# A fused attention and two-layer kernel: the first layer's w_out parts streamed from DRAM, and w_out2's combinations moved from GpSimd to VectorE

## The chip, the cores and the metric

The kernel runs on one core of one Trainium2 chip. The metric is the device time of one execution in microseconds (us). Of the kernel before, three runs are known: 1842.84, 1839.39 and 1833.98 us, median 1839.39. The trace is of one more execution, which took 1837.5 us.

The engines are named as in the profile: PE is TensorE's matmul side and PEld its weight loads, DVE is VectorE, ACT is ScalarE, POOL is GpSimd, SP is SyncE, which here does nothing but issue DMAs in order.

## The reference, cut to what matters

```python
# attention: 8 batches, 8 heads, 576 positions, head size 64; k and v averaged over groups of 8
k_p = k.reshape(B, H, Sp, pool, D).mean(axis=3)
v_p = v.reshape(B, H, Sp, pool, D).mean(axis=3)
attn = softmax(scale * q @ k_p.T)            # 576 x 72 for each head
x = (attn @ v_p)                             # rearranged to 4608 x 512

# first layer: w_in 512 x 2048, w_out 2048 x 512, stored as float64
h = x @ w_in
y = (h * np.cos(h)) @ w_out                  # 4608 x 512

# second layer: w_gate, w_val 512 x 1536, w_out2 1536 x 512, stored as float64
g = y @ w_gate
out = (g / (1 + np.exp(-g)) * (y @ w_val)) @ w_out2
```

## The kernel before, in words

**Precision.** Most matrix products are made of three fast matmuls: each operand is split into a high part (a copy rounded to the fast format, made by ScalarE) and a low part (the operand minus its high part, made by VectorE), and high x high, low x high and high x low are added up in PSUM. The weights come as float64 and are converted on VectorE by bit operations (the `cv_` functions).

**First layer.** The 4608 tokens are nine blocks (n = 0 to 8) of 512, the 2048 hidden columns sixteen groups (f = 0 to 15) of 128; one (n, f) is a *slot*, numbered i = 16 n + f, 144 in all. In a slot TensorE makes h (`pe_h`, L478 to L480, 12 matmuls of 512 columns) from x's parts `xhl` and w_in's parts `wa`, which stay on chip. ScalarE and VectorE then form h cos(h): `hs` (L487), `w` (L489, L490), sine and square (L501, L502), and the product (L505). `parts` splits it into `gh` (ScalarE, L517) and `gl` (VectorE, L519). Two slots later `pe_y` (L536 to L538, 12 matmuls) multiplies them with w_out's parts into four PSUM banks, `acc`. From slot 11 on w_out's row group f, which lies converted in two tiles `wo_raw` of eight groups each, is split again in every slot: the high part `woh` by ScalarE (`wo_high`, L495), the low part `wol` by VectorE (L518), each with two buffers in turn. At a block's last slot `x_split` splits the next block's x (4 copies on ScalarE, 4 subtractions on VectorE), and at the next block's second slot `y_out` sends y to DRAM (`y_dram`).

**Beside it.** Attention for the later batches, the sums over groups of 8 of k and v (GpSimd, L185 and L187, `do_raw`), and the conversion of the second layer's weights (36 units at the slots in `cv_slots`, stored to `w2_dram`) are placed in given slots.

**Second layer.** It is computed by a scheme of seven products (P1 to P7) on halves of rows and columns, which needs sums and differences of weight blocks. For w_out2 these are made once, in `gen_out`: for each of six pairs of 128-row tiles, `load` fetches them by eight strided DMAs (L676) into a tile `ow`; then come seven steps, one for a product: GpSimd makes the sum or difference (L701), ScalarE the high part (L703, L696), GpSimd the low part (L704; L697 and L698 for P4), and a DMA writes both to `wc_dram` (L706). Its 42 steps are written into the last block, four to a slot. The tiles `ow` lie in the places `tP6` and `tP7`, where operands of the second layer come later. `t_steps` and `gen_steps`, which make the first operands of the second layer, are in the last block too.

**What sets the order.** The program is written as one sequence, but a planner in the framework decides the order on each engine and on SP's queue when the kernel is built, by data and buffer dependencies and its own costs. An instruction can come earlier on its engine than it is written, as soon as its data and place are there. On the chip each engine then takes its list strictly in order; an instruction that waits holds up all behind it.

Of the kernel before, what the change touches and what calls it, by code (L numbers as in the profile page):

```python
# [8 lines left out]
F32 = mybir.dt.float32  # L9
F32R = mybir.dt.float32r  # L10
# [4 lines left out]
ALU = mybir.AluOpType  # L15
# [10 lines left out]
def fused_kernel(  # L26
# [18 lines left out]
    nc = tc.nc  # L45
# [56 lines left out]
    nc.gpsimd.memset(exp_bias, -896.0 * 2.0**23)  # L102
    nc.gpsimd.memset(magic, MAGIC)
    y_dram = dram.tile([KC, P, NT], F32, name="y_dram")
    w2_dram = dram.tile([3 * FF2 * DM // (P * TB), P, TB], F32, name="w2_dram")


# [16 lines left out]
    def split(hi, lo, src):  # L124
        nc.scalar.copy(hi, src)  # L125
        nc.vector.tensor_sub(lo, src, hi)  # L126
# [345 lines left out]
    def pe_h(s):  # L472
        n, f = s
        ps = psum.tile([P, TB], F32, name=f"h_{n}_{f}", tag="hg", bufs=2)
        j, o = f // 4, (f % 4) * P
        for c in range(KC):
            whi, wlo = wa[j, c][:, 0, o : o + P], wa[j, c][:, 1, o : o + P]
            nc.tensor.matmul(ps, whi, xhl[:, 0, c], start=c == 0, stop=False)  # L478
            nc.tensor.matmul(ps, whi, xhl[:, 1, c], start=False, stop=False)  # L479
            nc.tensor.matmul(ps, wlo, xhl[:, 0, c], start=False, stop=c == KC - 1)  # L480
        hps[s] = ps
# [9 lines left out]

    def wo_high(s):
        n, f = s
        a = wo[s] = p1w.tile([P, DM], F32R, name=f"woh_{n}_{f}", tag="woh", bufs=2)
        nc.scalar.copy(a, wo_raw[f // 8][:, f % 8])  # L495

    def cosine(s):
        n, f = s
        w, h = wsb[s], hsb.pop(s)

        nc.scalar.activation(w, w, AF.Sin, scale=PI)  # L501
        nc.scalar.activation(w, w, AF.Square, scale=SQRT2)  # L502
        if n:
            wo_high(s)
        nc.vector.scalar_tensor_tensor(out=w, in0=w, scalar=1.0, in1=h, op0=ALU.subtract, op1=ALU.mult, reverse0=True)  # L505

    def parts(s):
        n, f = s
        if n == 0 and f < Y32:
            return  # L510
        a = gh[s] = chain_tile("gh", f"gh_{n}_{f}", F32R)
        b = gl[s] = chain_tile("gl", f"gl_{n}_{f}", F32R)
        c = p1w.tile([P, DM], F32R, name=f"wol_{n}_{f}", tag="wol", bufs=2)
        w = wsb.pop(s)
        if not n:
            wo_high(s)
        nc.scalar.copy(a, w)  # L517
        nc.vector.tensor_sub(c, wo_raw[f // 8][:, f % 8], wo[s])  # L518
        nc.vector.tensor_sub(b, w, a)  # L519
        wo[s] = (wo[s], c)  # L520

    def pe_y(s):
        n, f = s
        if f == 0:
            acc[n] = [psum.tile([P, TB], F32, name=f"acc_{n}_{i}", tag=f"acc{i}") for i in range(4)]
        if n == 0 and f < Y32:
            g = wsb.pop(s)
            for i in range(KC):
                a = wo_raw[f // 8][:, f % 8, i * P : (i + 1) * P]
                nc.tensor.matmul(acc[n][i], a, g, start=f == 0, stop=f == NF1 - 1)  # L530
            return
        a, b = wo.pop(s)
        xh, xl = gh.pop(s), gl.pop(s)
        for i in range(KC):
            cols = slice(i * P, (i + 1) * P)
            nc.tensor.matmul(acc[n][i], a[:, cols], xh, start=f == 0, stop=False)  # L536
            nc.tensor.matmul(acc[n][i], a[:, cols], xl, start=False, stop=False)  # L537
            nc.tensor.matmul(acc[n][i], b[:, cols], xh, start=False, stop=f == NF1 - 1)  # L538
# [127 lines left out]
    def gen_out():  # L666

        work = {}

        def load(i):  # L670
            t = work[i] = pools2["a"].tile([P, 4, TB], F32, name=f"ow_{i}", tag=f"tP{6 + i % 2}")
            raw = t[:, :2].rearrange("p e (m c) -> p e m c", m=4)
            u = units.index(("o", i // 2, 2 * i))
            for e in range(2):
                for m in range(4):
                    nc.sync.dma_start(  # L676
                        raw[:, e, m].rearrange("p (a d) -> p a d", a=4),
                        w2_dram[u + e].rearrange("p (a m d) -> p m a d", a=4, m=4)[:, m],
                    )

        for i in range(NI):
            if i == 0:
                load(0)
            if i + 1 < NI:
                load(i + 1)
            t = work.pop(i)
            a11, a21, a12, a22 = (t[:, e, h * 256 : (h + 1) * 256] for e in range(2) for h in range(2))
            outs_ = [t[:, 2 + n].bitcast(F32R).rearrange("p (a c) -> p a c", a=2) for n in range(2)]
            for n, (prod, dst, x, y, op) in enumerate((
                ("P1", None, a11, None, None), ("P2", None, a12, None, None), ("P4", a11, None, None, None),  # L690
                ("P5", a22, a21, a22, ALU.add), ("P7", a21, a11, a21, ALU.subtract),
                ("P6", a11, a22, a11, ALU.subtract), ("P3", a12, a12, a11, ALU.subtract),
            )):
                o = outs_[n % 2]
                if prod == "P4":
                    nc.scalar.mul(o[:, 0], a22, -1.0)  # L696
                    nc.gpsimd.tensor_add(o[:, 1], a22, o[:, 0])  # L697
                    nc.gpsimd.tensor_scalar(o[:, 1], o[:, 1], -1.0, None, op0=ALU.mult)  # L698
                else:
                    if dst is not None:  # L700
                        nc.gpsimd.tensor_tensor(out=dst, in0=x, in1=y, op=op)  # L701
                        x = dst
                    nc.scalar.copy(o[:, 0], x)  # L703
                    nc.gpsimd.tensor_sub(o[:, 1], x, o[:, 0])  # L704
                k = NI * NQ + NJ * OUT_PRODUCTS.index(prod) + i // 2
                nc.sync.dma_start(  # L706
                    wc_dram[k].rearrange("p (a x) -> p a x", a=2)[:, i % 2], o.rearrange("p a c -> p (a c)").bitcast(F32)
                )
                yield

    def run(steps, m=1):
        for _ in range(m):
            next(steps, None)
# [332 lines left out]
    for i, s in enumerate(slots):  # L1046
        n, f = s
        if s == (NB - 1, 0):
            p1a.release()
            pools2["a"] = tc.alloc_tile_pool(name="p2a", bufs=1, reuse_waits="tile")  # L1050
            tsteps = t_steps(0)
            gsteps = None
        units1, units2 = units2, []
        if n == 0:
            if f % KC == 0:
                fill_to("i", f // KC, KC - 1)
            load_i(1)
        if i + 2 in cv_slots and i % NF1 != 1:
            w2_get()
        if f == 0 and i:  # L1060
            pe_y(slots[i - 2])
        pe_h(s)
        if n == 0:
            fill(4)
        turns(s)
        if 0 < i <= NF1:
            fill_to("o", 0, i - 1)
        if i:
            parts(slots[i - 1])
        if f == NF1 - 1 and n + 1 < NB:  # L1070
            x_split((n + 1) % 2)
        if n == 0:
            fill(2)
        for u in units1:
            cv_bias(u)
        if f == 1 and n:
            pe_y(slots[i - 2])
        run_slot(mids, i)
        if f > 1 or i == 1:
            if i >= 2:  # L1080
                pe_y(slots[i - 2])
        if n == 0:
            fill(2)
        cosine(s)
        if f == 1 and n:
            y_out(n - 1)
        for u in units1:
            nc.sync.dma_start(w2_dram[w2c], cv_val(u))
            w2c += 1
        run_slot(lates, i)  # L1090
        run_slot(exps, i)
        run_slot(norms, i)
        if n == 0:
            if i == 0:
                do_pt(0, 4)
                do_qt(1, 0)
                for p in range(NP):
                    do_av(0, 2, p)
            if i == 2:
                prep_v(1)  # L1100
        else:
            if i + 2 in cv_slots and i % NF1 == 1:
                w2_get()
            if i + 1 in cv_slots:
                units2 = [f"w2_{w2c}"]
        for u in units2:
            cv_exp(u)
        if n == NB - 1:
            if f == 1:
                load_x2(0)  # L1110
            if f == 2:
                gen_load(0)
            if f == 0:
                osteps = gen_out()
            run(osteps, 4)
            if 6 <= f < 14:
                run(tsteps)
            if f == 8:
                gsteps = gen_steps(0)
            if f >= 8:  # L1120
                run(gsteps, 2)
# [80 lines left out]
```

## Time and profile before

| | |
|---|---|
| runs, median (lowest to highest) | 1839.39 us (1833.98 to 1842.84) |
| profiled execution | 1837.5 us, its span 1835.8 us, mean granted TensorE clock 0.983 |
| TensorE matmul busy | 1730.7 us, 94% of the span |
| TensorE weight loads busy | 1447.6 us, 79% |
| VectorE busy | 1351.2 us, 74% |
| ScalarE busy | 1124.5 us, 61% |
| GpSimd busy | 295.7 us, 16% |
| DMA | 289.92 MB, mean 158 GB/s |

Busy time is the share of the span in which the engine had an instruction in execution; matmuls overlap, so that one of 512 columns lasts about 0.39 us in the trace while the next starts some 0.23 us after it. Attention for the first batch and the conversion of w_in fill the first 80 us; the first layer's slots start at about 82 us, slot 16 at 216, slot 32 at 326, slot 128 at 950.65, and its last matmuls end at about 1052; the rest is the second layer.

### The profile page before, as it was taken

Reading aid. Unit: us, or ns where it says so; the run is one execution under the profiler, and the core shown is the slowest. Engines: PE = TensorE matmul, PEld = TensorE weight load, DVE = VectorE, ACT = ScalarE, POOL = GpSimd, SP = SyncE. Lnnn points to the kernel's source line nnn. Section 1 sums busy time; section 2 is a strip of 40 time slices with the busy share of each in tenths; the row PEclk is TensorE's granted clock in tenths of the full one; section 3 lists DMA queues with packets and bytes.
Section 4 is the critical chain, followed back from the end, with each engine's and each line's share of the span. In section 5 each row is a group of like instructions: output and inputs, shape, how many; then the busy total and the mean of one; then the engine's idle time right before and its main releaser. Section 6 shows DMA issues by size and latency. Waiting matters only on the chain.

```text
span 1835.8 us, 23628 instructions
## 1 busy us (share of the span) xinstructions
PE 1730.7 (94%) x8084; PEld 1447.6 (79%) x8084; DVE 1351.2 (74%) x2242; ACT 1124.5 (61%) x2059; POOL 295.7 (16%) x365
## 2 busy tenths in 40 slices
PE   2579999999999999999888999999999999999998
PEld 2455777887878887888766878888888888999998
DVE  6989988978886888888878686863486368448447
ACT  3567877887867878888677764533353344334333
POOL 4371424215060050000455000000000000000000
PEclk9799999999999999999989999999999999999999
DMA  9833323233231141212664289567667666788783
GB/s 188 172 108 88 90 88 97 76 71 102 44 98 55 32 147 37 86 36 70 195 188 167 115 280 321 192 210 271 194 192 250 213 194 208 280 277 262 280 249 96
DMA packets 229728, 289.92 MB, mean 158 GB/s; under 512 B 147560, under 2 KB 153704, under 8 KB 229608
## 3 DMA queue, kind: packets, MB, share of 16 engines
q1 hardware_dynamic: 206108, 284.87, 49.8%
q10 hardware_dynamic: 23500, 3.54, 1.4%
q8 instruction: 64, 1.05, 0.2%
q14 instruction: 56, 0.46, 0.1%
HBM read 227.02 MB, written 61.34 MB: 157 GB/s over the span
## 4 chain that ended last, share of the span: by engine, by line
PE 64%; DVE 18%; ACT 6%; DMA 5%; issue 3%; POOL 2%; SPq 1%; ACTq 0%; DVEq 0%; POOLq 0%
PE X L720 14%; PE oX L850 8%; PE Y L720 7%; PE oY L850 4%; PE acc L537 4%; PE acc L536 4%; PE acc L538 4%; PE Z L720 4%; PE h L479 4%; PE h L478 4%; PE h L480 4%; PE oZ L850 2%; DVE w L505 2%; DVE w L490 2%; PE s L252 2%
## 5 line engine op out<-in xcount | busy, mean ns | idle before, releaser
L478 PE MATMUL h<-xhl,wa 128*128 128x512 f32 x576 | 230.2, 400 | 5.6 <-ACT hs L487 5.6
L720 PE MATMUL X<-t_P,wc 128*128 128x512 f32 (+1 forms) x1080 | 233.0, 368 | 2.0 <-ACT u L769 2.0
L536 PE MATMUL acc<-gh,woh 128*128 128x512 f32 x532 | 216.2, 410 | 14.9 <-ACT gh L517 14.8
L479 PE MATMUL h<-xhl,wa 128*128 128x512 f32 x576 | 226.5, 393 | 1.2 <-DVE xhl L126 1.2
L480 PE MATMUL h<-xhl,wa 128*128 128x512 f32 x576 | 225.2, 391 | 0.0
L537 PE MATMUL acc<-gl,woh 128*128 128x512 f32 x532 | 213.7, 402 | 11.6 <-DVE gl L519 11.5
L720 PEld LDWEIGHTS X<-t_P,wc 128*128 128x128 f32 x1080 | 196.5, 188 | 28.9 <-ACT u L769 3.8
L538 PE MATMUL acc<-gh,wol 128*128 128x512 f32 x532 | 211.5, 397 | 0.0
L501 ACT ACTIVATE w<-w 128x512 f32<-128x512 f32 x144 | 91.0, 632 | 68.4 <-DVE w L490 67.3
L536 PEld LDWEIGHTS acc<-gh,woh 128*128 128x128 f32 x532 | 101.7, 192 | 39.6 <-ACT gh L517 19.1
L537 PEld LDWEIGHTS acc<-gl,woh 128*128 128x128 f32 x532 | 102.0, 192 | 38.8 <-DVE gl L519 19.5
L478 PEld LDWEIGHTS h<-xhl,wa 128*128 128x128 f32 x576 | 109.2, 190 | 29.4 <-ACT hs L487 6.1
L479 PEld LDWEIGHTS h<-xhl,wa 128*128 128x128 f32 x576 | 108.8, 189 | 25.6 <-DVE xhl L126 2.4
L480 PEld LDWEIGHTS h<-xhl,wa 128*128 128x128 f32 x576 | 108.5, 188 | 23.5 <-issue 0.7
L505 DVE SCALAR_TENSOR_TENSOR w<-w,hs 128x512 f32<-128x512 f32 x144 | 107.7, 748 | 24.1 <-ACT w L502 23.5
L519 DVE TENSOR_TENSOR gl<-w,gh 128x512 fp32r<-128x512 f32 x133 | 99.8, 750 | 33.1 <-ACT gh L517 32.1
L772 DVE TENSOR_TENSOR p<-p,X 128x512 f32<-128x512 f32 (+1 forms) x60 | 37.9, 632 | 115.9 <-PE X L720 107.8
L538 PEld LDWEIGHTS acc<-gh,wol 128*128 128x128 f32 x532 | 102.0, 192 | 21.8
L487 ACT ACTIVATE hs<-h 128x512 f32<-128x512 f32 x144 | 85.7, 595 | 51.9 <-DVE w L505 35.9
L518 DVE TENSOR_TENSOR wol<-wo,woh 128x512 fp32r<-128x512 f32 x133 | 97.7, 735 | 25.0 <-ACT woh L495 22.0
L490 DVE SCALAR_TENSOR_TENSOR w<-w,hs 128x512 f32<-128x512 f32 x144 | 107.5, 747 | 10.5 <-ACT w L489 10.5
L125 ACT CAST xhl<-pst 128x1024 fp32r<-128x1024 f32 (+1 forms) x70 | 67.7, 968 | 72.0 <-PE oX L850 26.2
(189 smaller groups left out, 3758.9 us busy)
## 6 DMA issues: line engine op xcount, KB each, us to landing
wc<-wc_dram SPq DMA_DIRECT2D x273, 512.0 KB
wc_dram<-wc SPq DMA_DIRECT2D x42, 512.0 KB
wc_dram<-ow SPq DMA_DIRECT2D x42, 256.0 KB
y_dram<-yo SPq DMA_DIRECT2D x18, 512.0 KB
w_dram<-ce_w SPq DMA_DIRECT2D x36, 256.0 KB
st_i<-in_moe_w_in_dram SPq DMA_DIRECT2D x32, 256.0 KB
st_o<-in_moe_w_out_dram SPq DMA_DIRECT2D x16, 512.0 KB
vraw<-in_v_dram SPq DMA_DIRECT2D x60, 128.0 KB
```

Source lines behind the costliest of these rows:

```text
L478: nc.tensor.matmul(ps, whi, xhl[:, 0, c], start=c == 0, stop=False)
L479: nc.tensor.matmul(ps, whi, xhl[:, 1, c], start=False, stop=False)
L480: nc.tensor.matmul(ps, wlo, xhl[:, 0, c], start=False, stop=c == KC - 1)
L490: nc.vector.scalar_tensor_tensor(out=w, in0=w, scalar=MAGIC, in1=h, op0=ALU.subtract, op1=ALU.subtract)
L505: nc.vector.scalar_tensor_tensor(out=w, in0=w, scalar=1.0, in1=h, op0=ALU.subtract, op1=ALU.mult, reverse0=True)
L518: nc.vector.tensor_sub(c, wo_raw[f // 8][:, f % 8], wo[s])
L519: nc.vector.tensor_sub(b, w, a)
L536: nc.tensor.matmul(acc[n][i], a[:, cols], xh, start=f == 0, stop=False)
L537: nc.tensor.matmul(acc[n][i], a[:, cols], xl, start=False, stop=False)
L538: nc.tensor.matmul(acc[n][i], b[:, cols], xh, start=False, stop=f == NF1 - 1)
L720: nc.tensor.matmul(ps[:, :hb], w, t[:, x, c, :hb], start=first and c == 0 and n == 0, stop=c == 1 and n == 2, skip_group_check=not first,)
L850: nc.tensor.matmul(banks[key][m][:, :hb], u, x[:, b, i, :hb], start=first_ and j == i == k == 0, stop=j == NJ - 1 and i == 1 and k == 2, s ...
```

## The change

In blocks 0 (from slot 11 on) and 1, w_out's two parts are made as before, but in one tile `wo` with both parts, and in block 1 that tile is also written to a new DRAM tensor `wo_dram`. From block 2 (slot 32) on nothing is split any more: `wo_load` fetches both parts of one group (512 KB) into a ring of four places, one slot ahead in the program's order; the ring takes the place of `wo_raw`'s first tile. `gen_out`'s tile takes the place of the second and holds two pairs. Its combinations are made by VectorE (P4's low part in one instruction instead of two), and its steps are written one to a slot into slots 64 to 78, 104 to 118 and 127 to 141, two pairs to a window with one step for the loads. `t_steps` start three slots earlier in the last block.

```diff
+    wo_dram = dram.tile([NF1, P, 2, DM], F32, name="wo_dram")
...
     def wo_high(s):
         n, f = s
-        a = wo[s] = p1w.tile([P, DM], F32R, name=f"woh_{n}_{f}", tag="woh", bufs=2)
-        nc.scalar.copy(a, wo_raw[f // 8][:, f % 8])
+        wo[s] = p1w.tile([P, 2, DM], F32R, name=f"wo_{n}_{f}", tag="wo", bufs=2)
+        nc.scalar.copy(wo[s][:, 0], wo_raw[f // 8][:, f % 8])
+
+    wo_ring = []
+
+    def wo_load(i):
+
+        n, f = slots[i]
+        if not wo_ring:
+            wo_ring.append(p1w.tile([P, 4, 2, DM], F32R, name="wo_ring", tag="big0", bufs=1))
+        wo[n, f] = wo_ring[0][:, i % 4]
+        nc.sync.dma_start(wo[n, f].bitcast(F32), wo_dram[f])
...
-        if n:
+        if n == 1:
             wo_high(s)
...
-        c = p1w.tile([P, DM], F32R, name=f"wol_{n}_{f}", tag="wol", bufs=2)
...
-        nc.vector.tensor_sub(c, wo_raw[f // 8][:, f % 8], wo[s])
+        if n < 2:
+            nc.vector.tensor_sub(wo[s][:, 1], wo_raw[f // 8][:, f % 8], wo[s][:, 0])
         nc.vector.tensor_sub(b, w, a)
-        wo[s] = (wo[s], c)
+        if n == 1:
+            nc.sync.dma_start(wo_dram[f], wo[s].bitcast(F32))
...
     def gen_out():
         work = {}
+        home = p1w.tile([P, 2, 4, TB], F32, name="ow", tag="big1", bufs=1)
         def load(i):
-            t = work[i] = pools2["a"].tile([P, 4, TB], F32, name=f"ow_{i}", tag=f"tP{6 + i % 2}")
+            t = work[i] = home[:, i % 2]
...
         for i in range(NI):
-            if i == 0:
-                load(0)
-            if i + 1 < NI:
+            if i % 2 == 0:
+                load(i)
                 load(i + 1)
+                yield
...
                 if prod == "P4":
                     nc.scalar.mul(o[:, 0], a22, -1.0)
-                    nc.gpsimd.tensor_add(o[:, 1], a22, o[:, 0])
-                    nc.gpsimd.tensor_scalar(o[:, 1], o[:, 1], -1.0, None, op0=ALU.mult)
+                    nc.vector.scalar_tensor_tensor(
+                        out=o[:, 1], in0=a22, scalar=-1.0, in1=o[:, 0], op0=ALU.mult, op1=ALU.subtract
+                    )
                 else:
                     if dst is not None:
-                        nc.gpsimd.tensor_tensor(out=dst, in0=x, in1=y, op=op)
+                        nc.vector.tensor_tensor(out=dst, in0=x, in1=y, op=op)
                         x = dst
-                    nc.scalar.copy(o[:, 0], x)
-                    nc.gpsimd.tensor_sub(o[:, 1], x, o[:, 0])
+                    split(o[:, 0], o[:, 1], x)
...
         pe_h(s)
+        if 2 * NF1 <= i + 1 < len(slots):
+            wo_load(i + 1)
...
+        if i == 2 * NF1:
+            osteps = gen_out()
+        if 64 <= i < 79 or 104 <= i < 119 or 127 <= i < 142:
+            run(osteps)
         if n == NB - 1:
...
-            if f == 0:
-                osteps = gen_out()
-            run(osteps, 4)
-            if 6 <= f < 14:
+            if 3 <= f < 11:
                 run(tsteps)
```

## Rows read from the trace of the kernel before

**Rows 1.** The page: busy tenths of TensorE and GpSimd in 40 slices of the span.

```profile
PE   2579999999999999999888999999999999999998
POOL 4371424215060050000455000000000000000000
```

**Rows 2.** Stretch, length; busy us (count): PE, PEld, DVE, ACT, POOL; clock; DMA share; GB/s.

```profile
876.27:903.49 27.22, 27.22 (x122) 22.53 (x121) 26.02 (x42) 20.51 (x39) 7.62 (x8) 1.00 0.84 223
903.49:1005.70 102.21, 86.52 (x338) 66.70 (x336) 73.33 (x86) 69.19 (x139) 60.65 (x65) 0.92 0.54 173
```

**Rows 3.** Timeline of GpSimd: start, duration, instruction and count.

```profile
901.90 4.41 POOL L701 TENSOR_TENSOR ow<-ow 128x256 f32<-128x256 f32 x4
```

**Rows 4.** Timeline of VectorE, the same subtraction before and beside it.

```profile
898.36 0.68 DVE L519 TENSOR_TENSOR gl<-w,gh 128x512 fp32r<-128x512 f32 x1
...
905.64 1.22 DVE L519 TENSOR_TENSOR gl<-w,gh 128x512 fp32r<-128x512 f32 x1
```

**Rows 5.** Timeline of ScalarE; in brackets its idle time ahead and what ended it.

```profile
910.28 0.71 ACT L703 CAST ow<-ow 128x256 fp32r<-128x256 f32 x2 [4.72 <-POOL ow L701]
910.90 0.63 ACT L501 ACTIVATE w<-w 128x512 f32<-128x512 f32 x1
```

**Rows 6.** Waits of TensorE's matmuls, 903.49 to 1005.70: total us, times, longest.

```profile
PE acc L536 <- ACT gh L517: 10.7, 6, 4.4
PE acc L537 <- DVE gl L519: 5.0, 7, 1.4
```

**Rows 7.** Groups of VectorE's instructions, 903.49 to 1005.70: count, busy us, mean ns.

```profile
L505 DVE SCALAR_TENSOR_TENSOR w<-w,hs 128x512 f32<-128x512 f32 x13 | 12.2, 939 | 6.0 <-ACT w L502 6.0
L518 DVE TENSOR_TENSOR wol<-wo,woh 128x512 fp32r<-128x512 f32 x14 | 12.1, 863 | 9.5 <-ACT woh L495 7.0 <-PE acc L538 2.4
...
L126 DVE TENSOR_TENSOR wc<-w2r,wc 128x256 fp32r<-128x256 f32 x6 | 3.1, 537 | 0.0
```

**Rows 8.** The same view, 767 to 867, without GpSimd work.

```profile
L505 DVE SCALAR_TENSOR_TENSOR w<-w,hs 128x512 f32<-128x512 f32 x16 | 11.0, 688 | 3.1 <-ACT w L502 2.9
```

**Rows 9.** Busy time by stretch (columns as in rows 2): blocks 1 to 6.

```profile
216.00:326.00 110.00, 104.10 (x493) 84.10 (x492) 96.56 (x168) 85.80 (x152) 41.49 (x54) 1.00 0.31 87
326.00:431.00 105.00, 103.35 (x494) 85.76 (x493) 89.80 (x166) 86.11 (x152) 29.59 (x41) 0.98 0.28 78
431.00:537.30 106.30, 103.78 (x495) 85.78 (x495) 91.47 (x166) 85.03 (x146) 31.79 (x36) 0.98 0.28 79
537.30:635.80 98.50, 97.59 (x461) 80.59 (x460) 71.31 (x136) 77.17 (x132) 11.33 (x17) 1.00 0.20 52
635.80:740.80 105.00, 102.34 (x494) 84.36 (x493) 89.94 (x166) 85.00 (x150) 27.71 (x35) 1.00 0.29 81
740.80:840.20 99.40, 99.40 (x481) 83.40 (x480) 82.59 (x159) 83.64 (x147) 0.00 (x0) 1.00 0.19 59
```

**Rows 10.** Waits of TensorE's matmuls, 326 to 903.49 (columns as in rows 6).

```profile
PE acc L537 <- DVE gl L519: 3.5, 4, 1.2
PE acc L536 <- ACT gh L517: 2.4, 2, 1.9
```

**Rows 11.** Groups of instructions over the whole span: count, busy us, mean ns.

```profile
L518 DVE TENSOR_TENSOR wol<-wo,woh 128x512 fp32r<-128x512 f32 x133 | 97.7, 735 | 25.0 <-ACT woh L495 22.0 <-PE acc L538 2.4
...
L495 ACT CAST woh<-wo 128x512 fp32r<-128x512 f32 x133 | 81.0, 610 | 4.4 <-PE acc L537 4.1
...
L126 DVE TENSOR_TENSOR wc<-w2r,wc 128x256 fp32r<-128x256 f32 x72 | 29.3, 430 | 9.9 <-ACT wc L125 9.7
```

**Rows 12.** SP and GpSimd: two timeline rows; issues of L676 (min/median/max ns); a wait, 210 to 335.

```profile
404.34 9.02 SPq L159 DMA_DIRECT2D kraw<-in_k_dram  x4
...
408.55 1.61 POOL L185 TENSOR_TENSOR kraw<-kraw 72x256 f32<-72x256 f32 x2 [11.07 <-DMA kraw<-in_k_dram]
...
L676 SPq DMA_DIRECT2D ow<-w_dram x48: 518/629/2329, 877.0 to 978.2; - x48
...
SPq L159 <- POOL kp L187: 52.1, 10, 30.4
```

More of the change, by code (lines that the diff above doesn't have):

```diff
@@ L531, in pe_y @@
             return
-        a, b = wo.pop(s)
+        t = wo.pop(s)
+        a, b = t[:, 0], t[:, 1]
         xh, xl = gh.pop(s), gl.pop(s)
```

## The prediction

> **What bounds the kernel now.** I read the page first: TensorE's digit is 9 from the fourth slice of the span on, except in three slices (872 to 1010 us) where it falls to 8, and these are the three of GpSimd's last work, 4, 5 and 5 [rows 1]. So the kernel is bound by TensorE, and what can be won is the time in which TensorE is short of work.
>
> The second view cuts that place at slot borders [rows 2]. A slot of the first layer without attention work is 24 matmuls. Slots 118 to 122 (876.27 to 903.49) take 27.22 us for 5 x 24 = 120 matmuls: 0.2268 us each, 5.44 us a slot, granted clock 1.00. Slots 123 to 136 (903.49 to 1005.70) are 14 such slots, 336 matmuls, and should take 14 x 5.44 = 76.2 us. They take 102.2 us: **26.0 us too many**, part of it as a granted clock of 0.92 on average behind the pauses (a mix of 2.4 GHz and the lower level). GpSimd is busy for 60.65 us of it, with the combinations of w_out2.
>
> The timelines tell how. While GpSimd runs four L701 in a row [rows 3], VectorE's subtraction of 512 columns goes from 0.68 to 1.22 us [rows 4], and ScalarE, whose order is fixed, stands 4.72 us in front of a copy (L703) that wants GpSimd's result, with the next sine queued behind it [rows 5]. TensorE then waits for gh (10.7 us in 6 waits) and gl (5.0 us in 7) [rows 6]. Over these slots VectorE's L505 takes 939 ns [rows 7] against 688 in a stretch without GpSimd [rows 8].
>
> The same chain costs a little in the other blocks. Blocks 2 to 6 (326 to 840.2) leave TensorE idle for 1.65 + 2.52 + 0.91 + 2.66 + 0.00 = 7.7 us [rows 9]; most of what is named of it is gl and gh again [rows 10].
>
> **The change part by part.**
>
> *w_out2's combinations go from GpSimd to VectorE, spread over three times 15 slots.* Removed: all 72 GpSimd instructions of the stage, 42 ScalarE copies' waits on them, and the sharing with VectorE. Added on VectorE: per pair of tiles 7 products give 6 subtractions, 4 combinations and 1 negate-and-subtract, so 11 instructions, for 6 pairs 66, at 0.430 us for a 256-column subtraction (a like shape) 28.4 us; 9.5 us in each window of 15 slots, 0.63 us a slot [rows 11]. In slots 123 to 136 VectorE's 73.3 us [rows 2] become: less 14 L518 at 0.863 (12.1, [rows 7]), less the stretching of about 40 other instructions by 0.25 (10, from 939 and 688, [rows 7, 8]), plus 9.5, about 61 us; I add 6 us for second-layer operands that no longer wait for the ow tiles' places and come earlier: 67 of 76 us, 88%. Slots 118 to 122 ran at 26.02 of 27.22 us, 96%, with TensorE never idle [rows 2]. So the stall should go. What is late next is the split of the next block's x at slot 127, which falls between two blocks, and the odd copy that meets its partner late in a fixed order. Gain between 0 and 26.0 us; I take 22.5, leaving 3.5, since block 6, with the same split and no GpSimd work, leaves 0.00 [rows 9].
>
> *w_out's two parts are streamed from block 2 on.* Removed in 112 slots: a ScalarE copy of 0.610 us and a VectorE subtraction of 0.735 us [rows 11], 68 and 82 us of engines that are not the bound. On the path only the 7.7 us of blocks 2 to 6 answer to it: of the six waits named [rows 10] each has about one copy and one subtraction ahead in its queue, and 6 x about 0.65 (half the 1.35) is 4 us. Bounds 0 and 7.7; I take 4, not more, since the idle time follows GpSimd's pooling sums (29.6, 31.8, 11.3, 27.7 and 0.0 us in these blocks [rows 9]), and these stay. In slots 64 to 79 and 104 to 119 the 0.63 us that the combinations add to VectorE is paid by the 0.735 that goes: nothing either way.
>
> *The stream itself.* Each slot loads 512 KB into a ring of four. The load for slot i+1 can start once TensorE has done y of slot i-3; before y of i+1 come four h and three y, 7 x 2.72 = 19 us. The nearest landing in the trace: four loads of 144 KB, the first issued at 404.34, GpSimd starting on it at 408.55, 4.2 us [rows 12]; for 512 KB I estimate 6 us (368 KB more at the 223 GB/s of [rows 2]). That leaves 13 us. On SP's queue the loads now stand among all others: the sixteen strided loads of each window, 16 x 0.63 = 10 us [rows 12], fit in. The bandwidth fits too: 0.5 MB per 5.44 us is 96 GB/s on top of 173 [rows 2]. Two waits are new. TensorE waits for a load, and all of TensorE stands behind it; SP waits for TensorE to free a place in the ring, and behind it stand k, v and w2 loads, whose users (GpSimd's sums, conversions) have slots to spare. I take 0.5 us lost; bounds 0 and rival 3.
>
> *Block 1 writes the parts out.* 16 stores of 512 KB on SP, and the tile of slot s (two in turn) is free for slot s+2 only when its store has landed. The store can go about 1.5 us behind the copy (copy 0.61, subtraction 0.735), 11 us lie between s and s+2, 6 us to land: 3 to 4 us to spare for a queue that in this block stood up to 30.4 us on GpSimd [rows 12]. ScalarE would stand at the copy, with gh queued behind it and TensorE behind that. Block 1 already leaves TensorE idle 5.9 of 110 us [rows 9]. I take 1 us; bounds 0 and 16 (1 us in each slot).
>
> *Moved operand steps in block 8* (from slots 134 to 141 to 131 to 138): the trace has the second layer's first splits inside slots 123 to 136 already, so nothing; GpSimd's end there frees what they waited for, which I have counted as VectorE's time above.
>
> **Sum.** 22.5 + 4 - 0.5 - 1 = 25 us. The profiled execution took 1837.5 us (span 1835.8, 1.7 around it), 1.9 below the median of the runs: 1812.5 against 1837.5, 1814.4 against 1839.4. I say 1813.
>
> **The rivals.**
>
> 1. *Half of it: VectorE takes GpSimd's place as the late engine at 903 to 1006.* The planner pulls work forward as far as data allow (the combinations stand at slot 128 in the program, and their loads issue from 877.0 on [rows 12], in slot 118). For it: 88% leaves little room when a fixed order slips, and w2's last four conversions lie in slots 120 to 124. Against: slots 118 to 122 ran clean at 96%, and no copy waits for GpSimd any more. Half of 22.5 lost: 1824.
>
> 2. *Combinations pulled into GpSimd's pooling sums.* The first window's inputs are ready from slot 60, and 431 to 537.3 holds 31.79 us of GpSimd sums [rows 9], which stay. In [rows 7] a 256-column subtraction beside GpSimd took 537 ns on average against 430, and at the stretching of a 512-column one (0.54 us more) it would be 0.97: 22 instructions are 12 to 21 us, in place of some 8 L518 at 1.2 us; a gap of up to 11 us, all on TensorE if VectorE is full: 1812.5 + 11 = 1823.5. For it: that window is VectorE's 91.47 of 106.3 us. Against: the split of x is ahead in the program and the sums are over within ten slots. The Trainium skill says the same of the cause (SBUF — State Buffer, "Who interferes with whom": a VectorE instruction with two SBUF inputs contends with a GpSimd instruction that reads SBUF, so the order of issue and not the shape decides who waits); the trace agrees at 0.68 against 1.22 us, and by this rule moving work to VectorE cures only the stretch where GpSimd falls silent.
>
> 3. *Slower: the stream comes late.* SP issues in a fixed order. If a load of the stream is queued behind one for k or v that waits for GpSimd's sums (30.4 us the longest [rows 12]), it is late by the stand less the 13 us to spare, 17 us, and TensorE stops. GpSimd has four bursts of sums in blocks 2 to 5; two such stands are 34 us: 1846.5. It decides from a stand of 13 us on. For it: 52.1 us of such stands in 210 to 335 [rows 12]. Against: the long ones are there because nothing else was due on the queue; in a burst it issues four loads in 9.02 us [rows 12].
>
> 4. *Block 1's stores hold ScalarE*: 16 us instead of 1: 1827.5.
>
> 5. *Everything named goes*: 26.0 + 7.7 with the low clock behind it, and nothing is lost: 1803.
>
> That the change doesn't do what it says would be the planner leaving the combinations bunched behind slot 120; that is rival 1.
>
> **How the numbers follow.** Forecast (1805 to 1820) 0.58; rival 1 0.13, rival 2 0.08, rival 3 0.08, rival 4 0.06, rival 5 0.07. Half a per cent, 9.2 us, is about what a measurement of this kernel can tell from no change: faster is below 1830. The forecast, rivals 1, 2 and 5 and most of 4 lie there, but tails of 1, 2 and 4 added to each other pass it: faster 0.80, same 0.11, slower 0.09. The range from 1801 to 1829 holds the forecast, rivals 1, 2, 4 and 5 but for their tails.
>
> **What the profile after would show.** Right: no L697 to L704 on GpSimd and no GpSimd work after about 700 us; slots 123 to 136 in 76 to 81 us, L505 near 690 ns there; clock 1.00; blocks 2 to 6 with less than 5 us idle; no TensorE wait that ends on a load of the ring. Wrong: waits of TensorE on the ring's loads (rival 3), ScalarE waits at L495 or L496 on stores in block 1 (rival 4), gh and gl waits of more than 8 us behind slot 122 (rival 1), or VectorE instructions of the combinations beside GpSimd between 500 and 550 us with idle TensorE (rival 2). The prediction is wrong if the time is above 1830.

## The result, and the profile after

The changed kernel takes 1807.47 us, the median of four runs (1804.27 to 1810.16), against 1836.93 (1833.98 to 1842.84) for the kernel before on the same chip: a ratio of 0.9835, 95% interval 0.9803 to 0.9867. The forecast was 1813 against 1839. The profiled execution took 1807.2 us (span 1805.5), 30.3 less than the one before.

The page of the changed kernel, slices as in [rows 1]:

```profile
PE   2589999999999999999999999999999999999998
POOL 4371423304104013000000000000000000000000
```

The three 8s of TensorE and the digits of GpSimd under them are gone together. GpSimd's last work now lies in the sixteenth slice.

The slot borders of [rows 2] and [rows 9] in the changed kernel (columns as there): slots 118 to 122, 123 to 136, block 1, then blocks 2 to 6 one by one, and these five in one stretch.

```profile
868.76:895.99 27.23, 27.23 (x123) 22.53 (x121) 23.98 (x42) 18.84 (x32) 0.00 (x0) 1.00 0.84 256
895.99:974.91 78.92, 77.89 (x338) 62.75 (x336) 57.64 (x103) 58.44 (x108) 0.00 (x0) 1.00 0.70 231
213.97:325.35 111.38, 105.48 (x495) 85.45 (x494) 97.60 (x171) 86.33 (x152) 41.00 (x54) 0.98 0.55 178
325.35:426.81 101.46, 101.46 (x495) 84.74 (x493) 78.93 (x147) 78.26 (x135) 17.59 (x25) 1.00 0.48 142
426.81:530.76 103.95, 102.65 (x494) 84.64 (x493) 82.01 (x159) 79.75 (x136) 19.93 (x32) 1.00 0.60 174
530.76:627.51 96.75, 96.75 (x460) 80.73 (x459) 69.97 (x132) 73.48 (x125) 25.12 (x37) 1.00 0.61 189
627.51:731.00 103.49, 102.63 (x495) 84.76 (x494) 78.48 (x149) 76.41 (x135) 22.41 (x35) 1.00 0.55 166
731.00:832.70 101.70, 100.54 (x482) 83.21 (x481) 79.40 (x163) 78.33 (x144) 0.00 (x0) 1.00 0.59 184
325.35:832.70 507.35, 504.03 (x2420) 418.09 (x2419) 388.78 (x750) 386.23 (x672) 85.05 (x128) 1.00 0.56 171
```

Set beside the same borders of before, the 30.3 us divide so:

| stretch | before | after | gain |
|---|---|---|---|
| up to slot 16 | 215.8 | 214.0 | 1.8 |
| block 1 (slots 16 to 31) | 110.2 | 111.4 | -1.2 |
| blocks 2 to 6 (32 to 111) | 514.2 | 507.4 | 6.8 |
| slots 112 to 122 | 63.3 | 63.3 | 0.0 |
| slots 123 to 136 | 102.2 | 78.9 | 23.3 |
| slots 137 to 142 | 33.0 | 32.6 | 0.4 |
| from slot 143 on | 797.1 | 798.0 | -0.9 |

The first and last lines are work that both kernels do alike. Over all kernels below, slot 16 starts between 212.1 and 216.3 us and the rest from slot 143 takes 796.1 to 800.0, so differences of 2 to 4 us there are scatter.

TensorE's waits of the changed kernel, 895.99 to 974.91 (columns as in [rows 6]):

```profile
PE acc L550 <- DVE gl L530: 0.9, 2, 0.5
```

VectorE's groups in the same stretch (columns as in [rows 7]): one of the layer's own products, which was L505, and one of the combinations.

```profile
L516 DVE SCALAR_TENSOR_TENSOR w<-w,hs 128x512 f32<-128x512 f32 x14 | 9.7, 690 | 7.6 <-ACT w L513 7.3
L127 DVE TENSOR_TENSOR ow<-ow 128x256 fp32r<-128x256 f32 x11 | 4.5, 423 | 3.7 <-ACT ow L126 3.7
```

So 10.7 and 5.0 us of named waits became 0.9, and L505's 939 ns became 690, close to the 688 that it had without GpSimd [rows 6 to 8]. The gain of 23.3 has two halves, both in the windows: TensorE's idle time fell from 102.21 - 86.52 = 15.7 to 1.0 us, and its busy time from 86.5 to 77.9, with the granted clock from 0.92 to 1.00 (2.4 GHz throughout). Behind the pauses the clock had been lower too.

### The profile page after: what moved, and what is told of

It is laid out like the page before. It is cut to its first block, busy times and chain, and to the rows that moved or that the text cites. A ratio compares the mean times of both kernels' runs of the same rounds, so it can differ in the third digit from the quotient of the medians.

```text
span 1805.5 us, 23613 instructions
## 1 busy us (share of the span) xinstructions
PE 1721.2 (95%) x8084; PEld 1443.0 (80%) x8084; DVE 1284.0 (71%) x2196; ACT 1072.8 (59%) x1947; POOL 211.0 (12%) x293
## 4 chain that ended last, share of the span: by engine, by line
PE 66%; DVE 18%; DMA 7%; ACT 6%; issue 2%; SPq 1%; POOL 0%; ACTq 0%; DVEq 0%; POOLq 0%
PE X L734 14%; PE oX L864 8%; PE Y L734 7%; PE acc L550 4%; PE acc L551 4%; PE oY L864 4%; PE acc L549 4%; PE h L479 4%; PE h L481 4%; PE h L480 4%; PE Z L734 3%; PE oZ L864 2%; DVE w L516 2%; DVE w L491 2%; PE av L330 1%
## 5 line engine op out<-in xcount | busy, mean ns | idle before, releaser
L550 PE MATMUL acc<-gl,wo_ring 128*128 128x512 f32 x448 | 175.8, 392 | 2.3 <-DVE gl L530 2.3
L549 PE MATMUL acc<-gh,wo_ring 128*128 128x512 f32 x448 | 174.7, 400 | 1.0 <-ACT gh L527 0.9
L551 PE MATMUL acc<-gh,wo_ring 128*128 128x512 f32 x448 | 174.9, 390 | 0.0
L516 DVE SCALAR_TENSOR_TENSOR w<-w,hs 128x512 f32<-128x512 f32 x144 | 103.2, 716 | 45.7 <-ACT w L513 44.4
L491 DVE SCALAR_TENSOR_TENSOR w<-w,hs 128x512 f32<-128x512 f32 x144 | 106.3, 738 | 15.9 <-ACT w L490 15.7
L490 ACT ACTIVATE w<-hs,few 128x512 f32<-128x512 f32 x144 | 104.6, 726 | 6.2 <-DMA w_dram<-ce_w 4.8
L186 POOL TENSOR_TENSOR kraw<-kraw 72x256 f32<-72x256 f32 x96 | 85.4, 890 | 168.6 <-DMA kraw<-in_k_dram 164.8
L527 ACT CAST gh<-w 128x512 fp32r<-128x512 f32 x133 | 81.7, 615 | 35.6 <-DVE w L516 31.9
L864 PE MATMUL oX<-xhl,wc 128*128 128x512 f32 (+1 forms) x480 | 102.8, 368 | 0.0
```

What stands on the lines that cost most here:

```text
L490: nc.scalar.activation(w, h, AF.Identity, bias=magic)
L491: nc.vector.scalar_tensor_tensor(out=w, in0=w, scalar=MAGIC, in1=h, op0=ALU.subtract, op1=ALU.subtract)
L864: nc.tensor.matmul(banks[key][m][:, :hb], u, x[:, b, i, :hb], start=first_ and j == i == k == 0, stop=j == NJ - 1 and i == 1 and k == 2, s ...
```

## The experiments

Stretches are cut at the same slot borders throughout; windows have the columns of [rows 2]. The kernel before, run beside each group, took 1834.69 us (e1 to e4), 1835.35 (e5 to e8) and 1836.39 (the repeat and e9 to e11) in the median, so differences between groups are good to some 2 us.

**Engine and stream taken apart: e1, e2, e3.** e1 is the kernel before with only the combinations' engine changed:

```
-                    nc.gpsimd.tensor_add(o[:, 1], a22, o[:, 0])
-                    nc.gpsimd.tensor_scalar(o[:, 1], o[:, 1], -1.0, None, op0=ALU.mult)
+                    nc.vector.scalar_tensor_tensor(out=o[:, 1], in0=a22, scalar=-1.0, in1=o[:, 0], ...)
-                        nc.gpsimd.tensor_tensor(out=dst, in0=x, in1=y, op=op)
+                        nc.vector.tensor_tensor(out=dst, in0=x, in1=y, op=op)
-                    nc.scalar.copy(o[:, 0], x)
-                    nc.gpsimd.tensor_sub(o[:, 1], x, o[:, 0])
+                    split(o[:, 0], o[:, 1], x)
```

e3 is the changed kernel with the combinations, still on VectorE, bunched in the last block as before; e2 is e3 with them on GpSimd:

```
-        if i == 2 * NF1:
-            osteps = gen_out()
-        if 64 <= i < 79 or 104 <= i < 119 or 127 <= i < 142:
-            run(osteps)
...
+            if f == 0:
+                osteps = gen_out()
+            run(osteps, 4)
```

The rest of the edit puts the tile's place, its loads and the start of `t_steps` back as they were before.

> Only the combinations of w_out2 go from GpSimd to VectorE; they stay in the last block, and w_out is split in every slot as before. Theory A (GpSimd's sharing with VectorE and ScalarE's waits on GpSimd make the 26 us, but VectorE must have room for the work): from 903 to 1039 us VectorE's 73.3 + 22.3 us lose 11.5 of stretching and gain 66 x 0.43 = 28.4, so 112.5 us against the 108.9 that TensorE wants: about 1823 us (1818 to 1829), with GpSimd idle in the last block and gl or gh waits left there. Rival B (leaving GpSimd is the whole matter): 1814 or less.

> Only the stream: w_out's parts come from DRAM from block 2 on; the combinations stay on GpSimd, in the last block, in their old places. Theory A: blocks 2 to 6 give their 7 us, and the stage of slots 123 to 136 keeps most of its 26 us (18 to 22): about 1824 us (1818 to 1830). Rival C (the stream's relief of ScalarE and VectorE would have cured the stage too): 1814 or less.

> The changed kernel, but the combinations, on VectorE, stay in the last block, four steps to a slot, in their old places. Theory A: with w_out's subtractions gone VectorE has about 98 us to do in the 109 us of 903 to 1039: most of the gain, about 1811 us (1808 to 1816). Rival D (the spreading over three windows is what made room): 1818 or more.

| us | combinations on GpSimd | on VectorE, last block |
|---|---|---|
| no stream | 1834.7 (before) | 1815.0, ratio 0.9892 (0.9872 to 0.9913) |
| stream | 1824.8, 0.9948 (0.9934 to 0.9963) | 1807.6, 0.9858 (0.9835 to 0.988) |

The engine alone gives 19.7 us, the stream alone 9.9, both 27.1: nearly their sum. e1 came out between its two theories and closer to the rival, e2 as expected, e3 just below its range. In its trace, slots 123 to 136, the next six slots, and blocks 2 to 6:

```profile
896.91:977.64 80.73, 78.09 (x337) 62.57 (x336) 71.85 (x142) 66.81 (x134) 0.00 (x0) 1.00 0.68 216
977.64:1012.08 34.44, 32.98 (x145) 26.89 (x144) 24.16 (x42) 26.23 (x48) 0.00 (x0) 1.00 0.21 82
321.03:833.62 512.59, 506.15 (x2419) 420.02 (x2418) 424.28 (x788) 416.85 (x726) 98.83 (x128) 0.99 0.25 70
```

VectorE carries w_out's subtractions and all the combinations in the last block and is busy 89% of the first stretch, yet TensorE is idle only 2.6 us of it. I had reckoned that VectorE would be the late engine there, with 112.5 us to do in slots 123 to 142. It was not: it was busy for 71.85 + 24.16 = 96.0 us, as long as before (73.33 + 22.31) although 58 of the 66 combinations were added. Its other instructions there, 124 in both kernels, last 83.7 us if their durations are added up, against 100.7 before: the stretching beside GpSimd was 17 us and not the 11.5 that I took off. That and the eight combinations ahead of slot 123 are some 9 of the 16.5 us by which I was out; the rest has no name. Bunching was no part of it: the combinations ran in slots 119 to 137, and GpSimd's before in slots 119 to 136. The splits among them in e1:

```profile
L126 DVE TENSOR_TENSOR ow<-ow x36: 415/419/426, 877.5 to 981.0; 128x256 fp32r<-128x256 f32 x36
```

e2's blocks 2 to 6 and slots 123 to 136:

```profile
326.28:831.47 505.19, 503.53 (x2420) 418.28 (x2418) 373.14 (x706) 377.81 (x644) 83.74 (x128) 1.00 0.49 153
894.76:980.95 86.19, 79.47 (x337) 62.44 (x336) 51.80 (x71) 57.99 (x113) 42.41 (x47) 1.00 0.79 248
```

The stream gains 9 us in blocks 2 to 6. In the last block it also takes part of the stall, though some of that only moves behind: slots 123 to 142 are 86.2 + 42.1 = 128.3 us, where before they were 102.2 + 33.0 = 135.2 and with VectorE in e3 80.0 + 33.7 = 113.7. So the engine is worth 14.6 us there with the stream and 20 without it (135.2 against e1's 115.2): the overlap of the two edits.

e3's slots 123 to 136:

```profile
890.43:970.43 80.00, 78.30 (x337) 64.19 (x336) 60.88 (x116) 59.37 (x116) 0.00 (x0) 0.98 0.87 269
```

It ends at the time of the changed kernel, 1807.64 against 1807.47; by the ratios, 0.9858 against 0.9835 and 0.984 for its repeat, it is 3 to 4 us behind, within the intervals. Spreading the combinations over three windows gives at most that; the rival that it was needed falls.

**GpSimd, spread as in the change: e5.** The changed kernel with the first diff above turned round.

> The changed kernel, with the combinations back on GpSimd but in the three windows. Theory A (sharing and ScalarE's waits on GpSimd cost wherever they run): 1815 us (1810 to 1822), with VectorE's instructions near 0.9 us and TensorE idle where GpSimd works. Rival E (spreading alone cures it, whatever the engine): 1809 or less.

Measured 1816.35 (1814.63 to 1819.01), ratio 0.9897 (0.9882 to 0.9912). Blocks 2 to 6, and slots 123 to 136:

```profile
325.95:839.80 513.85, 506.57 (x2420) 419.08 (x2418) 384.03 (x706) 387.65 (x673) 125.73 (x176) 1.00 0.55 168
903.09:984.42 81.33, 78.92 (x337) 63.72 (x336) 54.69 (x82) 59.12 (x109) 20.54 (x23) 0.98 0.70 227
```

Spread out, GpSimd costs 2.4 us in the last stretch but 6.5 in blocks 2 to 6: the price moves with the work. In all it is 9 us against the changed kernel; e2, with the same work bunched, was 17 above e3.

**Which part of GpSimd's work costs: e4 and e8.** e4 was to take ScalarE's waits on GpSimd away from the kernel before by letting GpSimd make the high parts as well:

```
-                    nc.scalar.mul(o[:, 0], a22, -1.0)
+                    nc.gpsimd.tensor_scalar(o[:, 0], a22, -1.0, None, op0=ALU.mult)
...
-                    nc.scalar.copy(o[:, 0], x)
+                    nc.gpsimd.tensor_copy(o[:, 0], x)
```

> The kernel before, but GpSimd makes the high parts of the combinations too, so that ScalarE never waits for GpSimd. It parts the two ways in which GpSimd costs. If ScalarE's waits are the main one: 1820 to 1828 us, with VectorE's L505 still near 930 ns beside GpSimd. If the sharing with VectorE is the main one: 1835 us or more, since GpSimd has 42 instructions more.

Measured 1860.81 (1859.21 to 1862.85), ratio 1.0145 (1.0129 to 1.0162): slower by 26 us, and no clean test of sharing, since ScalarE still stood 14.88 us for GpSimd at an operand (`t_P`) that takes the place of an `ow` tile. Slots 123 to 136 took 128.37 us:

```profile
902.28:1030.65 128.37, 84.78 (x337) 66.36 (x336) 73.30 (x97) 61.74 (x109) 85.43 (x103) 0.84 0.46 149
```

Its timelines, SP's queue and then ScalarE, and the wait of TensorE that is left:

```profile
940.15 23.22 SPq L706 DMA_DIRECT2D wc_dram<-ow  x14
...
963.46 0.39 SPq L589 DMA_DIRECT2D ring<-y_dram  x1
...
971.93 1.04 ACT L125 CAST t_P<-ring 128x1024 fp32r<-128x1024 f32 x1 [25.11 <-DMA ring<-y_dram]
...
PE acc L536 <- ACT gh L517: 40.2, 3, 24.8
```

SP stands at the stores of parts that GpSimd, with 42 more instructions to do, has not made; the load of y behind them goes out 23 us late; ScalarE stands 25.11 us at the copy of it, in a fixed order with gh behind, and TensorE 24.8 us at gh. One late engine reached TensorE through two queues, although neither TensorE nor gh wants anything of it.

e8 asks the question cleanly. The changed kernel gets 70 GpSimd additions of 256 columns in slots 123 to 136 whose results nobody reads:

```
+        if i == 2 * NF1 + 2:
+            noise = p1w.tile([P, 2, DM], F32, name="noise", tag="wo", bufs=2)
+        if 123 <= i < 137:
+            t = wo[s][:, 0].bitcast(F32)
+            for j in range(5):
+                nc.gpsimd.tensor_tensor(out=noise[:, j % 2, :256], in0=t[:, :256], in1=t[:, 256:], op=ALU.add)
```

> The changed kernel plus 70 GpSimd additions of 256 columns, five to a slot in slots 123 to 136, whose result nobody uses and which read the ring: GpSimd busy beside VectorE, and no engine waits for it. Only the sharing is left. If the sharing alone makes the 26 us: 1820 us or more, VectorE's L516 near 930 ns there. Theory A (sharing and ScalarE's waits together, with VectorE at 73 percent): VectorE's instructions stretch, and TensorE loses 2 to 8 us: 1810 to 1815. If ScalarE's waits were all: 1809 or less.

Measured 1828.17 (1827.21 to 1829.3), ratio 0.9961 (0.9947 to 0.9975): 20.7 us above the changed kernel. The stretch, VectorE's products in it and the added instructions, and TensorE's waits:

```profile
898.49:996.24 97.75, 83.06 (x338) 64.50 (x336) 81.67 (x95) 55.45 (x101) 72.31 (x70) 0.97 0.55 183
...
L516 DVE SCALAR_TENSOR_TENSOR w<-w,hs 128x512 f32<-128x512 f32 x13 | 13.8, 1064 | 5.8 <-ACT w L513 5.4
L1082 POOL TENSOR_TENSOR noise<-wo_ring 128x256 f32<-128x256 f32 x70 | 72.7, 1070 | 217.4 <-DMA wo_ring<-wo_dram 217.0
...
PE acc L550 <- DVE gl L530: 7.9, 8, 2.7
PE acc L549 <- ACT gh L527: 6.8, 3, 4.0
```

The stretch is 18.8 us longer. L516 takes 1064 ns against 690, no ScalarE or VectorE instruction wants a result of GpSimd, and the two waits on the layer's own chain (14.7 us) are all of TensorE's idle time (97.75 - 83.06). A new order of the instructions is not the reason: from slot 32 to 142 VectorE, ScalarE and TensorE run theirs in the very order of the changed kernel. So sharing alone is enough for a loss of the size of the old one, and the theory that I held, that sharing costs only 2 to 8 us and the rest comes from ScalarE's waits on GpSimd, falls. How the old loss itself divides is not shown: GpSimd is busier here than before (72.31 against 60.65 us), VectorE too (81.67 against 73.33), and no run has ScalarE's waits alone, since e4 is no clean test. The Trainium skill (SBUF — State Buffer, "Who interferes with whom") states that a VectorE instruction with two SBUF inputs contends with a GpSimd instruction that reads SBUF; the rows agree, at 1064 against 690 ns. It also says that TensorE and ScalarE never wait on anyone there; TensorE's 14.7 us of waits in e8 end on gl and gh, which the slowed VectorE made late.

**w_out's work put back: e6.** The changed kernel, from block 2 on, with the copy and the subtraction that the stream saves, on another tile and with a result that nothing uses:

```
+            nc.scalar.copy(back[s][:, 0], wa[0, 0][:, 0])
...
+            nc.vector.tensor_sub(back[s][:, 1], wa[0, 0][:, 0], back.pop(s)[:, 0])
```

> The changed kernel, but from block 2 on ScalarE and VectorE make a copy and a subtraction of the same size in each slot, from a tile of w_in's parts, whose result nobody uses: the stream without its relief. Theory A (the 7 us of blocks 2 to 6 are the work that went): 1814 us (1811 to 1820), blocks 2 to 6 idle near 7 us again. Rival F (the 7 us come from the k and v sums, which moved in time behind the stream's loads): 1809 or less.

Measured 1821.29 (1821.21 to 1822.74), ratio 0.9925 (0.991 to 0.9939), 13.8 above the changed kernel: twice what was expected. Blocks 2 to 6, block 4, block 5, and VectorE's added subtractions:

```profile
326.40:848.97 522.57, 511.58 (x2419) 420.04 (x2418) 454.91 (x862) 438.92 (x784) 92.56 (x128) 0.99 0.54 166
537.27:644.82 107.55, 104.05 (x472) 83.61 (x471) 96.34 (x172) 90.74 (x162) 28.39 (x37) 0.98 0.59 178
644.82:747.37 102.55, 102.20 (x494) 84.66 (x493) 78.06 (x149) 76.66 (x135) 22.66 (x35) 1.00 0.55 167
...
L535 DVE TENSOR_TENSOR wb<-wa,wb x112: 632/684/1256, 327.9 to 600.3; 128x512 fp32r<-128x512 f32 x112
```

The stretch grew by 15.2 us. The added work was not spread as the w_out work of before had been: it depends on nothing in its slot, so that all 112 copies and subtractions ran in slots 32 to 73, 2.7 to a slot instead of one. The other instructions came in a new order too. Where they ran, in blocks 2, 3 and 4, TensorE took 2.3, 3.2 and 10.8 us longer than in the changed kernel; in blocks 5 and 6, where none were left, 0.9 and 0.1 us less. So such work costs TensorE time with the stream's loads in place, and the rival, that the gain came from the sums moving in time (1809 or less), falls; but neither the 13.8 nor the 15.2 us is a measure of the stream's gain. That is e2's 9.0 us in blocks 2 to 6.

**How deep the ring must be: e7 and e11.** e7 makes the ring two places instead of four. Part of its computation changes with that: the load of slot i+1 takes the place of slot i-1 before that slot's y is formed, so each y uses the parts of the group two slots on. e11 also moves the load behind y of slot i-2, which restores the computation:

```
-            wo_ring.append(p1w.tile([P, 4, 2, DM], ...))
+            wo_ring.append(p1w.tile([P, 2, 2, DM], ...))
-        wo[n, f] = wo_ring[0][:, i % 4]
+        wo[n, f] = wo_ring[0][:, i % 2]
...
-        if 2 * NF1 <= i + 1 < len(slots):
-            wo_load(i + 1)
+        if i >= 2 * NF1:
+            wo_load(i)
```

> The changed kernel with a ring of two places instead of four: a load can start when y of the slot two before is done, three half slots of 2.72 us = 8.2 us ahead of its use. If a load takes the estimated 6 us: a few stalls where it stands behind others on SP, 1810 to 1820 us. If loads take more than 8 us from release to landing: TensorE waits on the ring in most slots, 1850 us or more.

> The changed kernel with a ring of two places, and the load of slot i written behind y of slot i-2, so that each group is still read as it should be: three half slots, 8.2 us, lie between the release of a place and the use of its next load, instead of 19 us. If a load takes the estimated 6 us on its own: 1808 to 1815 us. If queueing on SP and transfer together often pass 8 us: TensorE waits on the ring by name, 1820 us or more.

e7: 1831.19 (1825.92 to 1836.87), ratio 0.9973 (0.9959 to 0.9988). e11: 1828.86 (1822.53 to 1831.49), 0.9955 (0.9941 to 0.9969). Both lose most of the gain: e7 lies between what its two theories gave, e11 in the range of its second, though with few of the waits that this theory wants. e11's blocks 2 to 6, one load and its first user, and TensorE's three longest waits there by name:

```profile
325.97:849.82 523.85, 510.06 (x2419) 418.29 (x2418) 390.86 (x750) 386.76 (x673) 88.46 (x128) 1.00 0.54 165
...
585.99 0.44 SPq L506 DMA_DIRECT2D wo_ring<-wo_dram  x1
...
590.18 0.47 PE L549 MATMUL acc<-gh,wo_ring 128*128 128x512 f32 x1 [1.07 <-DMA wo_ring<-wo_dram]
...
PE h L479 <- ACT hs L488: 6.8, 7, 1.7
PE acc L549 <- DMA wo_ring<-wo_dram: 4.3, 3, 2.9
PE acc L550 <- DVE gl L530: 1.7, 4, 0.7
```

A load that a matmul waited for was used 4.2 us after its issue, so the lead (two passes of h and one of y, 3 x 2.72 = 8.2 us) should do, and only 4.3 of 13.8 us idle end on the ring. The other idle time is on the layer's own chain, in an instruction order that also changed. Beside the repeat, blocks 2 to 6 lose 14.8 us and slots 123 to 136 lose 7.9 (86.0 against 78.1), where no wait of TensorE ends on the ring. Why two places cost 22 us is open; these runs don't tell a late load from the new order.

**Two ways to go further, beside a repeat: e9, e10.** The changed kernel run again beside them: 1806.31 (1805.59 to 1808.29), ratio 0.984 (0.9823 to 0.9858).

> The changed kernel once more, on the same chip as the next three: 1807 us (1804 to 1811), the ground on which they are compared.

e9 addresses a pause at slot 106 of the changed kernel, where a split waits for the store of the place that it writes, with gh behind it. The changed kernel's timeline of ScalarE, then TensorE:

```profile
790.27 0.41 ACT L126 CAST ow<-ow 128x256 fp32r<-128x256 f32 x1 [2.00 <-DMA wc_dram<-ow]
...
793.19 0.50 PE L549 MATMUL acc<-gh,wo_ring 128*128 128x512 f32 x1 [0.93 <-ACT gh L527]
```

```
-            outs_ = [t[:, 2 + n]... for n in range(2)]
+            outs_ = [home[:, k // 2, 2 + k % 2]... for k in range(4)]
-                o = outs_[n % 2]
+                o = outs_[(7 * i + n) % 4]
```

> The changed kernel, but the combinations write their parts into four places in turn instead of two, so that ScalarE's copy doesn't wait for the store of two steps before. If these waits (2.0 and 1.9 us on ScalarE at 788 and 918 us) are what slots 106 and 127 lose: 1.7 to 2.5 us less, 1805 us, and slot 106 of 5.5 us plus its attention work. If not: no change.

Measured 1805.42 (1804.92 to 1806.17), ratio 0.9834 (0.9817 to 0.9852). Slots 123 to 136 come close to the 76.2 us that their matmuls need, 1.6 below the repeat's 78.1 and 2.4 below the changed kernel's:

```profile
896.84:973.32 76.48, 76.47 (x337) 62.99 (x336) 57.26 (x103) 58.33 (x108) 0.00 (x0) 1.00 0.72 239
```

The total can't be told from the repeat: inconclusive as a time. Nor did the waits go: from block 2 to the first layer's end ScalarE stands 3.6 us in 2 waits at splits for stores of such places, against 4.2 in 3 in the repeat.

e10 moves the pooling sums of the later batches from GpSimd to VectorE as well:

```
-        pool_sum(nc.gpsimd, dst, kvraw.pop((b, kind, i)))
+        pool_sum(nc.vector if b > 3 else nc.gpsimd, dst, kvraw.pop((b, kind, i)))
```

> The changed kernel, with the k and v sums of batches 4 to 7 made by VectorE instead of GpSimd: about 63 us of VectorE work in blocks 2 to 6 (17 sums of 0.93 us for each batch), and GpSimd silent from block 2 on. If the sharing is what blocks 2 to 6 still lose and VectorE has room (389 of 507 us busy): 3 to 6 us faster than the changed kernel, 1802 us. Rival (VectorE gets full in the bursts, as it did at the last split of x): 1812 or more.

Measured 1802.52 (1800.76 to 1803.58), ratio 0.9817 (0.9799 to 0.9835), the fastest version. Its four runs lie below all of the repeat's, though the two intervals overlap. Block 1 and blocks 2 to 6 in e10, and then in the repeat:

```profile
214.38:321.68 107.30, 103.91 (x495) 85.61 (x494) 90.76 (x181) 85.72 (x152) 17.67 (x26) 0.98 0.52 173
321.68:827.15 505.47, 502.26 (x2419) 418.10 (x2418) 405.01 (x896) 385.84 (x673) 0.00 (x0) 1.00 0.56 174
```

```profile
214.00:327.40 113.40, 106.32 (x494) 86.03 (x493) 97.08 (x171) 87.01 (x153) 42.04 (x54) 0.98 0.55 177
327.40:836.47 509.07, 505.30 (x2420) 418.57 (x2418) 388.51 (x749) 386.04 (x672) 84.07 (x128) 1.00 0.55 170
```

VectorE has more instructions but is busy less in block 1 (90.76 against 97.08 us), since the rest of its work is stretched less: L516 takes 690 ns there against 762. Block 1 of the repeat is the longest of all, so part of its 6.1 us is scatter, and slots 123 to 136 take 80.3 us in e10 against 78.1. GpSimd's row shows the sharing gone from the seventh slice (270 us) on:

```profile
POOL 3351410000000000000000000000000000000000
```

## Why the prediction was right, step by step

- *Combinations to VectorE*: 22.5 predicted, 23.3 in slots 123 to 136. The 3.5 us left over were 2.7. e9, where 0.3 are left, does not settle what they are: of the 2.7, about 1.0 lie in slot 127, where ScalarE stands 1.85 us for a store of the combinations, and 1.0 in slot 130, ahead of which it stands 1.71 us for the load of y. VectorE's room was misjudged the safe way: 67 of 76 us forecast, 57.6 of 78.9 found, since the stretching was underpriced (e1: 17 us over slots 123 to 142 where the same reckoning took 11.5). e8 confirms the cause that [rows 4, 7] suggested, sharing, and shows that ScalarE's 4.72 us stand [rows 5] was not needed for it.
- *The stream's saved work*: 4 predicted, 6.8 found; this is the mis-sized term. I had counted only idle time: that fell from 7.7 to 3.3 us, 4.4 as forecast. The other 2.4 are TensorE's busy time, 506.46 to 504.03, as the clock of 0.98 in blocks 2 and 3 [rows 9] came back to 1.00 when the pauses went. The same stretch of before in one window:

```profile
326.00:840.20 514.20, 506.46 (x2419) 419.89 (x2418) 425.11 (x788) 416.94 (x726) 100.42 (x128) 0.99 0.25 70
```

  I priced the low clock in slots 123 to 136 and left it out here. That the sums' neighbourhood would stay as it was failed too: blocks 2 and 4 now have no idle time with the sums in them.
- *The stream's loads*: 0.5 predicted; no wait of TensorE ends on the ring. SP's waits in the changed kernel, whole span:

```profile
SPq L506 <- PE acc L551: 213.2, 64, 8.9
SPq L163 <- POOL vp L188: 28.7, 13, 10.6
SPq L160 <- POOL kp L188: 47.7, 21, 7.3
```

  SP stands 213 us for places in the ring, 8.9 at most at a time, and no wait of TensorE leads back to it; the longest stand on GpSimd is 10.6, under the 13 from which rival 3 decides. My 6 us for a landing was too long if e11's 4.2 stands for the others. The stands did reach ScalarE, which the forecast left out: a store of converted weights, ready at 655.4, goes out at 658.05 behind three loads of the ring, and ScalarE stands 3.45 us for the place that it frees (tiles `w` and `ce_w` share four places). There are two such waits, 4.8 us in all, and none before. TensorE stayed busy from 658 to 672.

```profile
649.10 8.03 SPq L506 DMA_DIRECT2D wo_ring<-wo_dram  x3
...
658.05 0.42 SPq L1104 DMA_DIRECT2D w_dram<-ce_w  x1
...
664.09 0.72 ACT L490 ACTIVATE w<-hs,few 128x512 f32<-128x512 f32 x1 [3.45 <-DMA w_dram<-ce_w]
```

- *Block 1's stores*: 1 predicted, 1.2 found, but not from the stores: ScalarE has no wait on them (rival 4 falls). TensorE's idle time there is 5.9 us as before, and the rest is a clock of 0.98 for 1.00. The ten profiles with the stream and all sums on GpSimd have 109.9 to 113.4, mean 111.9; the three without the stream 109.0 to 110.2: what the stream adds to this block, its stores and the new tile, costs some 2 us, by no wait with a name; that it is the stores is not shown.
- *Rival 1* falls: 0.9 us of gl waits where it needed over 8. *Rival 2* happened in place but not in price: the splits ran beside GpSimd's sums, at up to 959 ns,

```profile
L127 DVE TENSOR_TENSOR ow<-ow x36: 373/421/959, 427.6 to 926.4; 128x256 fp32r<-128x256 f32 x36
```

  and blocks 2 to 6 are 505.7 to 509.1 us in the three profiles of the changed kernel, its repeat and e9, against 503.7 and 505.2 in e3 and e2, where no combination is in them: 1 to 5 us where it priced 11. Nor is all of that beside GpSimd: the changed kernel's block 6, where GpSimd does nothing, takes 101.7 us against 99.4 in e3. *Rival 5* nearly came: 1807 for its 1803; e10 is there.
- The terms found, 23.3 + 6.8 - 1.2 and 0.4 behind, make 29.3; the medians differ by 29.5. The forecast had 25; errors of opposite sign did not cancel, and most of the difference is the stream's 2.8.

## What to carry to other kernels

Work on GpSimd that reads SBUF is not free because nobody waits for it: price it as time added to VectorE's instructions while it runs, and if VectorE has room (here 73 to 89% busy in slots 123 to 136 with the work on it), move it there before you spread or reorder it. Price a stall with the clock: idle time removed gave back about half as much again in busy time (8.6 on 14.7 us, 2.4 on 4.4). Not all of that need be the clock: in e8 busy time rose by 5.2 us at a clock of 0.97, which over 97.75 us is worth 2.9 at most. A load that stands in an in-order queue is harmless until something with less lead is behind it, so look for what is queued there and not at the length of the stand.

## What the runs showed that was not expected

- Work that nobody waits for, 70 GpSimd additions of 256 columns at 1.07 us, cost a stretch bound by TensorE 18.8 us (e8).
- VectorE at 89% busy did not hold TensorE up (2.6 us idle in 80.7, e1).
- A late GpSimd result cost TensorE 24.8 us in one piece by way of SP's queue and ScalarE's order (e4).
- A ring of two, with loads that a matmul could use 4.2 us after issue, cost 22 us more than a ring of four (e11); the cause stays open.
